# A two-layer product behind a retention block: two levels of Strassen for the first product of four chunks

## The chip, the cores and the metric

One NeuronCore of one Trainium2 chip runs one program. The metric is the time of that program on the device in microseconds. The engines are TensorE (PE, with its weight loads listed apart as PEld), VectorE (DVE), ScalarE (ACT), GpSimd (POOL) and the DMA queues, which SyncE (SP) issues.

## What is computed

All tensors are fp32; the weights arrive as 64-bit floats and are converted on the chip.

```python
q, k, v: (4, 8, 768, 64)          # batch, heads, time, head dim
w_in: (512, 2048)   w_out: (2048, 512)

for t in range(S):                # retention, one decay gamma[h] per head
    state = gamma * state + outer(k[:, :, t], v[:, :, t])
    y[:, :, t] = scale * q[:, :, t] @ state
x = y.transpose(0, 2, 1, 3).reshape(3072, 512)
h = x @ w_in                      # first product
g = maximum(0.01 * h, h)          # leaky relu
return g @ w_out                  # second product
```

## The kernel before

**Chunks and units.** Time is cut into NC = 6 chunks of C = 128 steps. A chunk has 4 batches, thus 512 tokens, which the products take as two halves of N = 256 columns. The 2048 hidden features are cut into NU = 4 units of 512. `hidden(c, u, ...)` (L615) makes unit u of the first product for chunk c, and `output(c, o, parts, ...)` (L650) adds the second product of one or two units into the chunk's output tile `o`.

**One level of Strassen.** Each product is a 2 by 2 block product in the form with seven products, M1 to M7, and three differences of either side. `seven` (L561) issues the matmuls: each of the seven has four of 128x128 weights by 256 columns, so a call has 28 for one unit and 56 for a pair. The sums go to four PSUM banks A to D, each a tile of its own (tag "ff", four buffers): M1 and M2 share A, M6 and M7 share B, M5 and M3 share C, M4 has D. After each of the seven, `takes` evacuates or adds: a ScalarE copy for M1 and M5, VectorE adds (`plus`, L526) for the others, a ScalarE leaky relu for each quarter of `g`. `differences` (L544) makes the three differences of `x` or `g` on VectorE. Weight sums (`add_sums`, L532) are made once on VectorE and stay in SBUF.

**Attention.** `reads`, `last_values`, `state`, `first_values` and `score` put 64-column and 128-column matmuls of the retention block into a pair of banks (`two_banks`, L158, tag "att", two buffers). `visit_with_scores` (L380) does two batches of a chunk in one go, with the scores of the two batches that come next.

**Order.** The schedule is written by hand: each engine executes its instructions in the order in which the code issues them. Chunks 0 and 1 go unit by unit while the weights still arrive and are converted (`round_piece`, L480). Chunks 2 to 5 then run `hidden`, `hidden`, `output` of the pair, twice a chunk, with the attention of the next chunk between. SP issues every load and store in program order, so a DMA that waits holds back those behind it.

Of the kernel before, what the change touches and what calls it, by code (L numbers as in the profile page):

```python
# [21 lines left out]

@with_exitstack
def kernel(
# [14 lines left out]

# [12 lines left out]
        tc.tile_pool(name="psum", bufs=2, space=bass.MemoryType.PSUM))  # L75

# [6 lines left out]

# [5 lines left out]
    def unit_tile(k, name):  # L91
        if k in LATE:
            return work.tile([128, 7, 2, 256], FP32, tag=f"late{k}", name=name)
        return const.tile([128, 7, 2, 256], FP32, name=name)
# [21 lines left out]

# [50 lines left out]

# [15 lines left out]
    def new_am(c, b):  # L187

        i = turn[0]
        turn[0] = (i + 1) % (3 if (c, b) >= (2, 2) else 2)  # L190
        if i < 2:
            return work.tile([128, 2, HP // 2, 3, C // 2], FP32, tag=f"am{i}", name=f"am_{c}_{b}")
        place = new_t(1, f"am_{c}_{b}").rearrange("p i k n -> p (i k n)")[:, 0 : 2 * NS]
        return place.rearrange("p (j m n t) -> p j m n t", j=2, n=3, t=C // 2)

    def new_t(c, name):
        return work.tile([128, 3, 2, N], FP32, tag=f"t{int(c == 1)}", name=name)
# [13 lines left out]


    pairs = [(j, m, i, 2 * m + i) for m in range(HP // 2) for j in range(2) for i in range(2)]

    def reads(c, b):
        x = heads[c, b][0]
        ps = sums_at[c, b] = two_banks(f"yp_{c}_{b}")
        for j, m, i, a in pairs:
            mm = nc.tensor.matmul(ps[ts(i, 64), j, m, :], lhsT=st[b][ts(j, 64), a, :],  # L219
                                  rhs=x[ts(j, 64), 0, a, :], start=(m == 0), stop=False,  # L220
                                  skip_group_check=True)


        reads_done[c, b] = nc.gpsimd.memset(between, 0.0).ins
        tc.add_manual_dep(reads_done[c, b], mm.ins.name, IN_ORDER, reason="rows of the array")
# [48 lines left out]
    def first_state(b, ps):  # L274


        y = heads[0, b][1]
        sp = ps[:, b // 2].rearrange("p a t -> p (a t)")[:, ds(b % 2 * HP * D, HP * D)]
        for a in range(HP):
            sums_of(sp.rearrange("p (a d) -> p a d", d=D), y, a, start=(b % 2 == 0 and a == 0))  # L280
# [35 lines left out]
    def ahead(c, b):  # L316


        if c >= NC:
            return  # L320
        if b < 2:
            x = work.tile([128, 2, HP, C], FP32, tag="qk", bufs=AHEAD, name=f"qk_{c}_{b}")
        else:
            if b == 2:
                room[c] = new_o(0).rearrange("p i k n -> p (i k n)")
            x = room[c][:, ds((b - 2) * 2 * HP * C, 2 * HP * C)]
            x = x.rearrange("p (s a t) -> p s a t", s=2, a=HP)
        heads[c, b] = [x, None]
        load_qk(c, b)
# [8 lines left out]
    def score_apart(c, b):  # L338

        banks = [psum.tile([128, HP * C], FP32, tag="ff", bufs=4, name=f"ap{j}_{c}_{b}")[:, 0:NS]  # L340
                 for j in range(2)]
        scores[c, b] = [ps.rearrange("p (m n t) -> p m n t", n=3, t=C // 2) for ps in banks]
        scores_to(heads[c, b][0], scores[c, b])
# [14 lines left out]
    def states_apart(c, b):  # L358

        ps = psum.tile([128, 2, HP, D], FP32, tag="ff", bufs=4, name=f"sp_{c}_{b}")  # L360
        for i in range(2):
            y = heads.pop((c, b + i))[1]
            for a in range(HP):
                sums_of(ps[:, i], y, a, start=(i == 0 and a == 0))
        return ps

    def visit(c, b):

        for f in (reads, last_values, state, first_values):
            for i in range(2):  # L370
                f(c, b + i)
        for i in range(2):
            tokens_taken(c, b + i, xs[c][0])
        for i in range(2):
            state_taken(c, b + i, for_state(sums_at[c, b + i]))
        for i in range(2):
            if c + 1 < NC:
                ahead(c + 1, b + i)

    def visit_with_scores(c, b, following, complete=False):  # L380

        x = xs[c][0]
        early, late = ((following[0], following[1] + i) for i in range(2))
        score_apart(*early)
        for i in range(2):
            reads(c, b + i)
        masked_apart(*early, 0)
        masked_apart(*early, 1)  # L390
        score_apart(*late)
        for f in (first_values, last_values):
            for i in range(2):
                f(c, b + i)
        masked_apart(*late, 0)
        for i in range(2):
            tokens_taken(c, b + i, x)
        sp = states_apart(c, b)
        if complete:
            if xs[c][1] is None:  # L400
                xs[c][1] = new_t(c, f"t_{c}")
            t = xs[c][1]
            for k in range(2):
                minus(t[:, 0, k], x[:, 1, k], x[:, 0, k])
                minus(t[:, 1, k], x[:, 3, k], t[:, 0, k])
        masked_apart(*late, 1)
        if complete:
            minus(t[:, 2], x[:, 2], t[:, 1])
        for i in range(2):
            state_added(c, b + i, sp[:, i])  # L410
        if complete:
            last_difference(x)
        for i in range(2):
            state_decayed(c, b + i)
        for i in range(2):
            ahead(c + 1, b + i)
        for at in (early, late):
            load_kv(*at)
        for at in (early, late):
            decay_v(*at)  # L420

# [67 lines left out]

# [3 lines left out]

# [7 lines left out]


# [50 lines left out]

# [5 lines left out]
    def seven(tiles, name, takes, takes_piece=None, order=ORDER):  # L561

        banks = {}
        which = [("M1", "A", 0, 0), ("M6", "B", 5, 5), ("M5", "C", 4, 4), ("M4", "D", 3, 6),
                 ("M2", "A", 2, 2), ("M7", "B", 1, 1), ("M3", "C", 6, 3)]
        for m, bank, sa, sb in (which[i] for i in order):
            first = bank not in banks  # L570
            split = takes_piece is not None and bank == "C"
            if first and split:
                two = [two_banks(f"{bank}{i}_{name}")[:, 0].rearrange("p a t -> p (a t)")
                       for i in range(2)]
                two.append(psum.tile([128, 2 * N], FP32, tag="ff", bufs=4, name=f"{bank}_{name}"))
                banks[bank] = [ps[:, 0 : z - a] for ps, (_, a, z) in zip(two, PIECES)]
            elif first:
                banks[bank] = psum.tile([128, 2, N], FP32, tag="ff", bufs=4, name=f"{bank}_{name}")
# [19 lines left out]
    def direct(c, u, x, g, th):  # L598


        banks = [psum.tile([128, 2, N], FP32, tag="ff", bufs=4, name=f"d{r}_{c}_{th}")
# [48 lines left out]
    def output(c, o, parts, first, final):  # L650
# [48 lines left out]
        def takes_piece(ps, i, a, z):  # L699
# [4 lines left out]
                     takes_piece if final and c == NC - 1 else None)  # L704

# [4 lines left out]
    def new_x(c):  # L710
        x = tile_x(c)
        return [x, new_t(c, f"t_{c}") if c < 3 else None]
# [76 lines left out]


# [3 lines left out]


    idle = psum.tile([128, 2, N], FP32, tag="ff", bufs=4, name="idle")
# [7 lines left out]

    tables = psum.tile([128, 2, N], FP32, tag="ff", bufs=4, name="tables")
    spread = psum.tile([128, 2, N], FP32, tag="ff", bufs=4, name="spread")
# [71 lines left out]


# [38 lines left out]


    for u in range(NU):
        for c in range(2) if u > 0 else ():
            if c == 0:
                parts = []
            parts.append(new_g(c, u))
            run(hidden(c, u, *xs[c], *parts[c][1:]), rounds(1, 3))
        for c in range(2):
# [5 lines left out]
            if u == NU - 1 and NC > 2:  # L934
                if c == 0:
                    xs[2] = new_x(2)
                if c == 0:
                    at = {0: [scored(2, 0), scored(2, 1)], 3: [lambda: visit(2, 0)]}
                else:
                    at = {1: [lambda: ahead(2, 2), lambda: ahead(2, 3)],  # L940
                          2: [lambda: load_kv(2, 2), lambda: load_kv(2, 3)],
                          4: [scored(2, 2), scored(2, 3)]}
            run(output(c, os[c], [parts[c]], u == 0, u == NU - 1), at)

    if NC > 2:
        visit_with_scores(2, 2, (3, 0), complete=True)
    for c in range(2, NC):
        os[c] = new_o(c)
        for p in range(NU // 2):
            pair = []  # L950
            for u in (2 * p, 2 * p + 1):
                pair.append(new_g(c, u))
                run(hidden(c, u, *xs[c], *pair[-1][1:]), {})
            last = p == NU // 2 - 1
            at = {}
            if c + 2 == NC and last:
                at = {3: [lambda: visit(c + 1, 2)], 5: [differ(c + 1)]}
            run(output(c, os[c], pair, p == 0, last), at)

            if c + 1 < NC and p == 0:  # L960
                xs[c + 1] = new_x(c + 1)
                visit_with_scores(c + 1, 0, (c + 1, 2))
            elif c + 2 < NC and last:
                visit_with_scores(c + 1, 2, (c + 2, 0), complete=True)
# [3 lines left out]

# [5 lines left out]

def _decay(H, D):

# [13 lines left out]

# [33 lines left out]

# [30 lines left out]
```

## Time and profile before

| what | value |
|---|---|
| median of 3 runs | 657.06 us (657.01 to 657.62) |
| profiled execution, its span | 655.4 us |
| instructions of PE / DVE / ACT / POOL | 4937 / 590 / 323 / 45 |
| busy time of DVE, ACT, POOL | 361.5, 176.1, 22.7 us |
| one add of 128x512 on DVE | 0.68 to 0.69 us |
| one copy of 128x512 from PSUM on ACT | 0.58 to 0.59 us |
| HBM read, written | 41.97 MB, 6.29 MB |

The span runs from the first to the last instruction of the profiled execution. An fp32 matmul stands in the trace as two records, each with a weight load of its own. A record lasts longer than its distance to the next one (379 ns beside 216 ns for 256 columns), since they are pipelined; the distance is what a matmul costs. "Idle before" is what an engine waited, with the engine that ended the wait.

### The profile page before, as it was taken

To read this page: it belongs to the slowest core of one execution; us is meant where nothing else is said; L and a number is where in the kernel's file an instruction comes from. 1 tells how busy PE (TensorE), PEld (TensorE's weight loads), DVE (VectorE), ACT (ScalarE), POOL (GpSimd) and SP (SyncE) were. 2 spreads that over 40 slices of the span, in tenths; PEclk is the share of its full clock that TensorE was granted. 3 is DMA by queue.
4 is the path that set the end of the run, shared out by engine and by line. 5 is a ranking of instruction groups with operands and counts; after the bars stand their busy time and mean duration, and the time that the engine had idled before them with its cause. 6 is when DMAs were issued, how large, how long until landed. Compare 5 with 4: busy or idle time off the path is not lost.

```text
span 655.4 us, 11361 instructions
## 1 busy us (share of the span) xinstructions
PE 650.6 (99%) x4937; PEld 568.2 (87%) x4937; DVE 361.5 (55%) x590; ACT 176.1 (27%) x323; POOL 22.7 (3%) x45
## 2 busy tenths in 40 slices
PE   8999999999999999999999999999999999999998
PEld 5888888888888888888888889888888888888887
DVE  5789969889887664243436414527423344431342
ACT  5855464264261003102102211300220210221210
POOL 1000000000000020000001001001000100000000
DMA  9921312323322650030022003005001001000001
GB/s 337 406 98 37 125 64 97 97 66 111 115 78 82 243 179 0 1 129 2 1 103 91 1 1 130 1 17 179 0 1 61 5 1 49 17 0 1 1 0 65
DMA packets 15906, 49.00 MB, mean 75 GB/s; under 512 B 1768, under 2 KB 2152, under 8 KB 15856
## 3 DMA queue, kind: packets, MB, share of 16 engines
q1 hardware_dynamic: 15696, 47.72, 20.7%
q8 instruction: 39, 0.64, 0.4%
q10 hardware_dynamic: 160, 0.55, 0.2%
q14 instruction: 11, 0.09, 0.0%
HBM read 41.97 MB, written 6.29 MB: 74 GB/s over the span
## 4 chain that ended last, share of the span: by engine, by line
PE 98%; DMA 1%; DVE 0%; ACT 0%; SPq 0%; issue 0%
PE B_o L585 13%; PE A_o L585 13%; PE C_o L585 13%; PE A_h L585 12%; PE B_h L585 12%; PE C_h L585 12%; PE D_o L585 6%; PE D_h L585 6%; PE ap L182 2%; PE d L607 2%; PE yp L255 2%; PE yp L219 1%; DMA raw<-in_weights_dram 1%; PE yp L244 1%; PE sp L270 1%; PE yp L270 0%
## 5 line engine op out<-in xcount | busy, mean ns | idle before, releaser
L585 PE MATMUL A_h<-x,w 128*128 128x256 f32 x368 | 87.7, 381 | 0.0
L585 PEld LDWEIGHTS A_h<-x,w 128*128 128x128 f32 x368 | 69.3, 190 | 9.6
L585 PE MATMUL A_o<-g,w 128*128 128x256 f32 x288 | 68.1, 379 | 0.0
L527 DVE TENSOR_TENSOR m<-m,B_h 128x512 f32<-128x512 f32 x23 | 15.8, 686 | 93.3 <-PE B_h L585 93.3
L585 PEld LDWEIGHTS A_o<-g,w 128*128 128x128 f32 x288 | 54.6, 190 | 7.5
L620 ACT ACTIVATE g<-g 128x512 f32<-128x512 f32 x69 | 42.0, 630 | 66.3 <-DVE g L527 66.3
L625 ACT COPY m<-A_h 128x512 f32<-128x512 f32 x23 | 13.5, 585 | 169.3 <-PE A_h L585 149.0
L527 DVE TENSOR_TENSOR m<-m,B_o 128x512 f32<-128x512 f32 x16 | 11.0, 685 | 64.4 <-PE B_o L585 64.4
L585 PE MATMUL B_h<-t,w 128*128 128x256 f32 x184 | 43.7, 380 | 0.0
L585 PE MATMUL C_h<-x,w 128*128 128x256 f32 x184 | 43.5, 379 | 0.0
L585 PE MATMUL C_h<-t,w 128*128 128x256 f32 x184 | 43.5, 379 | 0.0
L585 PE MATMUL D_h<-t,w 128*128 128x256 f32 x184 | 43.5, 379 | 0.0
L585 PE MATMUL B_h<-x,w 128*128 128x256 f32 x184 | 43.5, 379 | 0.0
L585 PEld LDWEIGHTS B_h<-t,w 128*128 128x128 f32 x184 | 34.7, 190 | 5.2 <-DVE t L530 0.6
L585 PEld LDWEIGHTS C_h<-x,w 128*128 128x128 f32 x184 | 35.0, 190 | 4.8
L585 PEld LDWEIGHTS D_h<-t,w 128*128 128x128 f32 x184 | 35.0, 190 | 4.8
L585 PEld LDWEIGHTS C_h<-t,w 128*128 128x128 f32 x184 | 35.0, 190 | 4.8
L585 PEld LDWEIGHTS B_h<-x,w 128*128 128x128 f32 x184 | 35.0, 190 | 4.8
L585 PE MATMUL C_o<-gd,w 128*128 128x256 f32 (+1 forms) x148 | 34.2, 373 | 0.0
L585 PE MATMUL C_o<-g,w 128*128 128x256 f32 (+1 forms) x148 | 34.2, 373 | 0.0
L530 DVE TENSOR_TENSOR gd<-g,gd 128x512 f32<-128x512 f32 x48 | 33.2, 692 | 1.7
L585 PE MATMUL B_o<-gd,w 128*128 128x256 f32 x144 | 34.1, 380 | 0.0
(131 smaller groups left out, 984.6 us busy)
## 6 DMA issues: line engine op xcount, KB each, us to landing
raw<-in_weights_dram SPq DMA_DIRECT2D x31, 512.0 KB, 3.9
kv<-in_kv_dram SPq DMA_DIRECT2D x17, 512.0 KB, 5.0
out_dram<-o SPq DMA_DIRECT2D x23, 256.0 KB, 2.1
qk<-in_qk_dram SPq DMA_DIRECT2D x10, 512.0 KB, 4.6
o<-in_qk_dram SPq DMA_DIRECT2D x8, 512.0 KB, 4.9
in<-in_qk_dram SPq DMA_DIRECT2D x5, 512.0 KB, 8.4
in<-in_kv_dram SPq DMA_DIRECT2D x3, 512.0 KB, 7.9
kv<-in_kv_dram SPq DMA_DIRECT2D x4, 256.0 KB, 7.4
```

Of the source, the lines that this page charges most:

```text
L182: nc.tensor.matmul(to, lhsT=x[ts(j, 64), 1, a, ts(late, 64)], rhs=x[ts(j, 64), 0, a, late * 64 :])
L219: mm = nc.tensor.matmul(ps[ts(i, 64), j, m, :], lhsT=st[b][ts(j, 64), a, :], rhs=x[ts(j, 64), 0, a, :], start=(m == 0), stop=False, skip_g ...
L244: mm = nc.tensor.matmul(ps[ts(i, 64), j, m, 0:64], lhsT=y[ts(s, 64), 1, 2 * a + j, :], rhs=am[ts(s, 64), j, m, 0], start=False, stop=True, ...
L255: nc.tensor.matmul(ps[ts(i, 64), j, m, 64:], lhsT=y[:, 1, 2 * a + j, :], rhs=am[:, j, m, 1 + (i ^ j)], start=(c == 0 and m == 0), stop=Tru ...
L270: nc.tensor.matmul(sp[ts(j, 64), a, :], lhsT=y[:, 0, 2 * a + j, :], rhs=y[:, 1, 2 * a + j, :], start=start, stop=True, skip_group_check=True)
L527: nc.vector.tensor_tensor(out=out, in0=a, in1=b, op=ALU.add)
L530: nc.vector.tensor_tensor(out=out, in0=a, in1=b, op=ALU.subtract)
L585: nc.tensor.matmul(to, lhsT=block(w, sa)[:, k, ts(i, 128)], rhs=rhs[:, k, a:z], start=(first and (i == 0 or split) and n == 0 and k == 0), ...
L607: nc.tensor.matmul(banks[r][:, i, :], lhsT=block(2 * u, r + 2 * kh)[:, k, ts(i, 128)], rhs=x[:, 2 * kh + th, k, :], start=(step == 0 and i ...
L620: nc.scalar.activation(g[:, i], g[:, i], AF.Prelu, alpha=0.01)
L625: nc.scalar.copy(out=got["m1"], in_=ps)
```

## The change

The first product of chunks 2 to 5 goes from one to two levels of Strassen. `hidden` is used there no more; `inner` and `outer` take its place, in two groups: group 0 makes four of the seven outer products, group 1 the other three. In `inner` each outer product is again seven products, each one matmul of 128x128 weights by 128 columns, so a group has 28 or 21 matmuls. All of it goes to one PSUM tile, `whole`, of four banks: the bank is the quarter of the inner result, the place in the bank is the outer product. A ScalarE copy puts M1 from bank 0 into bank 3, onto which later matmuls accumulate; three VectorE adds per group finish the inner sums in PSUM. `outer` does what `takes` did.

The second weight sums are made on GpSimd from the first while chunks 0 and 1 run (`sums_of_unit`), stored to DRAM (`keep_unit`), and loaded for each chunk and unit again (`load_unit`, 14 KB and 10.5 KB a partition, in two transfers each, into `wa` and `wb`). `output` is called unit by unit and takes its four banks from two tiles of two banks each (`att_banks`). The attention uses `joint_visit`, with its scores in `whole`. The main loop handles unit n of the second product while unit n+1 of the first is made.

```diff
-    def seven(tiles, name, takes, takes_piece=None, order=ORDER):
+    def att_banks(name):
+        ab, cd = (two_banks(f"{n}_{name}").rearrange("p j a t -> p j (a t)") for n in ("ab", "cd"))
+        return [ps.rearrange("p (i n) -> p i n", i=2)
+                for ps in (ab[:, 0], ab[:, 1], cd[:, 0], cd[:, 1])]
+    def seven(tiles, name, takes, takes_piece=None, order=ORDER, room=None):
...
+            elif first and room is not None:
+                banks[bank] = at[bank]
             elif first:
-                banks[bank] = psum.tile([128, 2, N], FP32, tag="ff", bufs=4, name=f"{bank}_{name}")
+                banks[bank] = ffs.tile([128, 2, N], FP32, tag="ff", bufs=4, name=f"{bank}_{name}")
...
+    def joint_visit(c, b, following):
+        for f in (reads, last_values, state, first_values):
             for i in range(2):
                 f(c, b + i)
+        ahead_of = [(following[0], following[1] + i) for i in range(2)] if following else []
+        for i, at in enumerate(ahead_of):
+            score_apart(*at, banks=[whole[:, q] for q in (2 * i, 2 * i + 1)])
         for i in range(2):
+            tokens_taken(c, b + i, xs[c][0])
+        for at in ahead_of:
+            for j in range(2):
+                masked_apart(*at, j)
         for i in range(2):
+            state_taken(c, b + i, for_state(sums_at[c, b + i]))
+            heads.pop((c, b + i))
...
+    def sums_of_unit(u):
...
+        for to, p, q, op in ((s1, a21, a22, ALU.add), (s2, s1, a11, ALU.subtract),
+                             (s4, a12, s2, ALU.subtract), (s3, a11, a21, ALU.subtract)):
+            nc.gpsimd.tensor_tensor(out=to, in0=p, in1=q, op=op)
...
+    def keep_unit(u):
+        for j, part in enumerate(to_keep.pop(u)):
+            nc.sync.dma_start(out=kept[u][:, j], in_=part)
...
+    whole = ctx.enter_context(
+        tc.tile_pool(name="whole", bufs=1, space=bass.MemoryType.PSUM)).tile(
+            [128, 4, 4 * C], FP32, name="whole")
+    regions = whole.rearrange("p q (i n) -> p q i n", i=4)
...
+    INNER = {"M1": (0, 0), "M2": (1, 1), "M4": (2, 4), "M5": (3, 2), "M6": (4, 3), "M3": (5, 5),
+             "M7": (6, 6)}
+    BANK = {"M1": 0, "M2": 0, "M5": 1, "M3": 1, "M4": 2, "M6": 3, "M7": 3}
+    N2 = (NC - 2) * NU
...
+    def load_unit(n, group):
...
+        if group == 0:
+            nc.sync.dma_start(out=wa[:, :, 0:1], in_=kept[u][:, :, 0:1])
+            nc.sync.dma_start(out=wa[:, :, 1:4], in_=kept[u][:, :, 3:6])
+        else:
+            nc.sync.dma_start(out=wb[:, :, 0:2], in_=kept[u][:, :, 1:3])
+            nc.sync.dma_start(out=wb[:, :, 2:3], in_=kept[u][:, :, 6:7])
...
+    def sums_of_x(c, group):
...
+            minus(made[:, 0], b12, b11)
+            minus(made[:, 1], b22, made[:, 0])
+            minus(made[:, 2], b21, made[:, 1])
+            minus(b12, b22, b12)
+    ORDERS = (("M1", "M5", "M6", "M4", "M2", "M7", "M3"), ("M1", "M5", "M4", "M6", "M2", "M3", "M7"))
+    def inner(n, group):
+        c, u = at_of(n)
+        w, count = ((wa, 4), (wb, 3))[group]
+        moving = operands(c, group)
+        def of(q):
+            return regions[:, q, 0:count]
+        t2, t3, t5 = e2[:, 0:count], e3[:, 0:count], e5[:, 0:count]
+        for m in ORDERS[group]:
+            j, s = INNER[m]
+            q = BANK[m]
+            for i, (block, sums) in enumerate(moving):
...
+                nc.tensor.matmul(regions[:, q, i], lhsT=w[:, j, i], rhs=rhs,
+                                 start=(i == 0 and m in ("M1", "M5", "M4")), stop=True,
+                                 skip_group_check=True)
+            if m == "M1":
+                nc.scalar.copy(out=of(3), in_=of(0))
+            elif m == "M5":
+                nc.scalar.copy(out=t5, in_=of(1))
+            elif m == "M6":
+                nc.scalar.copy(out=t2, in_=of(3))
+            elif m == "M7":
+                nc.scalar.copy(out=t3, in_=of(3))
+        load_unit(n + 1, group)
+        plus(of(3), of(3), t5)
+        plus(of(2), of(2), t3)
+        plus(of(1), of(1), t2)
+    def outer(n, group):
+        if group == 0:
+            nc.scalar.copy(out=m1, in_=regions[:, :, 0])
+            plus(u2, m1, regions[:, :, 3])
+            nc.scalar.copy(out=m5, in_=regions[:, :, 2])
+            nc.scalar.copy(out=m4, in_=regions[:, :, 1])
+            plus(u5, u2, m5)
+            return
+        gs[n] = new_g(*at_of(n))
+        g = gs[n][1]
...
+        plus(to(0), m1, regions[:, :, 1])
+        leaky(0)
+        plus(u2, u2, regions[:, :, 0])
+        plus(to(1), u5, regions[:, :, 2])
+        leaky(1)
+        plus(to(3), u2, m5)
+        leaky(3)
+        plus(to(2), u2, m4)
+        leaky(2)
...
+    for group in range(2):
+        load_unit(0, group)
+    x, t = xs[2]
+    differences(x, t)
+    sums_of_x(2, 0)
+    sums_of_x(2, 1)
+    for b in range(2):
+        ahead(3, b)
+        load_kv(3, b)
+        decay_v(3, b)
...
+    last = output(1, os[1], [parts[1]], False, True, room=att_banks)
+    products(last, 3)
+    for i in range(2):
+        score_apart(3, i, banks=[whole[:, q] for q in (2 * i, 2 * i + 1)])
+        for j in range(2):
+            masked_apart(3, i, j)
+    for b in range(2):
+        ahead(3, 2 + b)
+    fill()
+    inner(0, 0)
+    outer(0, 0)
+    products(last, 2)
+    inner(0, 1)
+    outer(0, 1)
+    products(last, 2)
+    for n in range(N2):
...
+        if more:
+            differences(*gs[n][1:])
+        if u == NU - 1 and more:
+            sums_of_x(c + 1, 1)
+        if more:
+            inner(n + 1, 0)
+            outer(n + 1, 0)
+        if c + 1 < NC and u < 2:
...
+                joint_visit(c + 1, 0, (c + 1, 2))
...
+        steps = output(c, os[c], [gs.pop(n)], u == 0, u == NU - 1,
+                       room=att_banks if more else whole_banks, order=ORDER if more else FIRST)
+        products(steps, 4)
+        if c + 1 < NC and u < 2:
+            fill()
...
+        if more:
+            inner(n + 1, 1)
+            outer(n + 1, 1)
+        if n + 2 == N2:
+            differences(*gs[n + 1][1:])
+        products(steps, 3)
```

`products(steps, n)` issues the next n of the seven products of `output`; `fill` is one bf16 matmul of 512 columns into bank 3 of `whole`.

## The prediction

> **What bounds the kernel now.** I read the busy shares first, then stretches without attention, then the pace of matmuls by shape.
>
> ```profile
> PE 650.6 (99%) x4937; PEld 568.2 (87%) x4937; DVE 361.5 (55%) x590; ACT 176.1 (27%) x323; POOL 22.7 (3%) x45
> ```
>
> TensorE is busy for 99% of the span, and the chain that ended last is 98% PE. In a stretch of chunk 2 without attention (view of stretches; columns: PE, PEld, DVE, ACT, POOL):
>
> ```profile
> 291.00:338.00 47.00, 47.00 (x219) 41.37 (x219) 18.97 (x31) 7.77 (x13) 2.08 (x2) 1.00 0.09 32
> ```
>
> PE has no gap, DVE works 40% and ACT 17% of it. So only TensorE's time counts, and a wait put before a matmul is paid in full unless other matmuls stand ahead of it in PE's order. The pace (timeline of PE, first 256 columns, then 128):
>
> ```profile
> 337.22 1.03 PE L585 MATMUL C_o<-g,w 128*128 128x256 f32 x4
> 338.08 1.03 PE L585 MATMUL C_o<-g,last_s 128*128 128x256 f32 x4
> ```
>
> ```profile
> 650.66 0.61 PE L585 MATMUL C_o<-g,w 128*128 128x128 f32 x4
> 651.10 0.61 PE L585 MATMUL C_o<-g,last_s 128*128 128x128 f32 x4
> 651.55 0.61 PE L585 MATMUL C_o<-g,w 128*128 128x128 f32 x4
> 652.00 0.61 PE L585 MATMUL C_o<-g,last_s 128*128 128x128 f32 x4
> ```
>
> Four records of 256 columns start 0.86 us apart, thus 216 ns each; four of 128 columns 0.446 us apart, thus 111.5 ns, each with its own 128x128 weight load. Halving the columns halves the price: weight loads do not bound the new shape. An fp32 matmul is two records: 0.432 and 0.223 us.
>
> **What the change removes on PE.** Per chunk and unit the first product goes from 28 matmuls of 256 columns (12.10 us) to 28 + 21 of 128 (6.24 + 4.69 = 10.93 us): 1.17 us less, 16 times, **-18.7 us**. The second product keeps its 28 matmuls a unit, and the attention its number. Seven `fill` matmuls come in, 0.25 us each with weight load: **+1.8 us**.
>
> **What it adds: turns.** In the order of the changed program with the wait that each instruction carries, the matmuls of `inner` do not only wait for what they need. `whole` is one tile, and after each ScalarE access to it the next matmul into it waits, whichever bank it writes. In group 0, M5 waits for the copy after M1, M6 for the copy after M5, M4 for that after M6, M3 for that after M7: four turns PE to ACT to PE with nothing ahead of them. Group 1 has three (M5, M4, M2). In `output` the banks A, B are one tile and C, D another: M6 waits for the copy after M1, M4 for the add after M5, M7 for the add after M2. Before, each bank was a tile of its own, and the copies lay beside the next product.
>
> One turn, from rows:
>
> ```profile
> L625 ACT COPY m<-A_h 128x512 f32<-128x512 f32 x23 | 13.5, 585 | 169.3 <-PE A_h L585 149.0
> L527 DVE TENSOR_TENSOR m<-m,B_h 128x512 f32<-128x512 f32 x23 | 15.8, 686 | 93.3 <-PE B_h L585 93.3
> L620 ACT ACTIVATE g<-g 128x512 f32<-128x512 f32 x69 | 42.0, 630 | 66.3 <-DVE g L527 66.3
> ```
>
> A record outlasts its pace by 0.16 us (275 - 111.5, or 379 - 216 ns); ACT or DVE starts 0.04 us after its end; the matmul starts 0.055 us after the release (as `d` at L607 after the DVE row on w), and the weight load, no longer hidden, shows as 0.104 us (that first record is 320 ns from the next, not 216). So a turn costs its operation plus 0.36 us. The copy of 512: 0.585 + 0.36 = 0.945 us. Of 384, on the line between 12 columns (0.168 us) and 512: 0.48 + 0.36 = 0.84. An add on DVE: 1.05. No row shows ACT or DVE writing PSUM: a copy there costs between the 0.168 us of the 12-column copy and the 0.63 of the leaky relu, an add between the 0.553 us of the 384-column mask and the 0.95 of the 768-column one. I take the same-sized rows.
>
> **One step of the loop without attention** (n = 2, 3, 6, 7 and on). Two waits are longer than a turn, since they stand behind a queue.
>
> - `inner` group 0: 4 x 0.945 = 3.8 us.
> - `output` M6 waits for the copy of M1, which is fourth in ACT's order. From the end T of group 0: 0.2, three adds in PSUM (2.07), copy m1 (0.62), add u2 (0.72), copies m5 and m4 (1.2), the copy itself (0.58), release 0.16: T + 5.56. M1 alone covers 1.73: 3.8 us.
> - M4 behind DVE's add: 1.05 us.
> - `inner` group 1: 3 x 0.84 = 2.5 us.
> - M7 waits for DVE's add of M2. From the end of group 1: 0.2, ACT's copy 0.48, three adds of 384 (1.66), five of `outer` (3.45), the add (0.69), release 0.16: 6.67 us. M2 alone covers 1.73: 4.9 us.
>
> Together 16.1 us of idle PE beside 23.0 us of work: a step of 39.1 us. Fifteen steps: 241.5 us. In the four first steps of a chunk M2 goes through ACT behind a leaky relu: +0.5 each. In the six steps with attention the scores wait for `outer`'s copy m4 (about 1.2 us), M1 of `output` for masks and states (3.0), while M6 falls to 0.95: 1.5 us more than without, each. **Stalls of the loop: +252 us.**
>
> **The change-over** (end of chunk 1). Weights of unit 0 are issued behind the last store of output(0, 3). By DMA rows (27 ns for 512 B, 48 for 1 KB, 16 engines) they take 9.5 us, and the qk and kv of chunk 3 stand behind them on SP: the second score can start about 20 us after the visit, of which M3, M1, M6 and M5 cover 8. With its mask 14 us of idle. Then the turns and waits of the first `inner` pair (3.8 + 1.5 + 2.5), M6's 0.95, and a slow clock of some 2 us: **+25 us**, between 12 (qk lands early) and 35. **The end**: the last M7 of step 14 stands behind four differences (+3), and the last `output` has four turns in `whole` (+4): **+7 us**.
>
> **Hidden.** Weight loads in the loop: 3.2 MB a step, 9.5 us by the packet rows (24 at the 131 GB/s of a raw load, 512 KB in 3.9 us), issued some 29 us ahead of their use. DVE has 17.5 us of adds a step of 39: late only where named. GpSimd's sixteen sums of 896 columns (1.9 us each from the 1.09 us of 512) and the stores fall into chunks 0 and 1, where DVE is busy 43.7 of 50 us; an add beside a GpSimd operation took 684 ns, beside none 686. I cost them at nothing; if raw loads are held behind the stores, up to 10.
>
> **The clock.** The trace shows what an idle PE does to it:
>
> ```profile
> 1.05 4.45 PE L800 MATMUL idle<-t 128*128 128x512 bf16 x10 [1.05 <-DVE t L764]
> 12.26 0.39 PE L800 MATMUL idle<-t 128*128 128x512 bf16 x1
> ```
>
> The first ten are 427 ns apart, twice the later pace of such columns (256 fp32 columns in two passes: 216), for at least 4.4 us: one re-warming costs 2.2 us. The trace has no gap of 3 to 5 us in mid-run; the longest near it, 0.4 us before `d`, left the clock high. Two gaps of each step (3.8 and 4.9 us) may trigger it: 0 to 30 x 2.2 = 66 us. The seven turns near 0.9 us resemble the 0.4 us gap; so I take few events, one of the longer gaps in three: **+12 us**.
>
> The Trainium skill ("TensorE: Matmul & The Clock Gate", Part 1) says that a free-running window of 3.4 us without work sets the clock to half until a busy one has passed. By that a 4.9 us gap holds such a window in 4 of 10 cases and a 3.8 us gap in 1 of 10; at an estimated 1.7 us each the sum would get 13 us instead of 12. The same skill ("PSUM — Partial Sum Buffer", PSUM bank collisions) asks engines to be kept apart bank by bank only; by that rule most turns are needless and the sum would be near that of the first rival. The waits are in the program, though, and the hardware obeys them.
>
> **Sum.** 655.4 - 18.7 + 1.8 + 252 + 25 + 7 + 12 = 934.5 us of span; the median stands 1.7 above the span: **936 us**.
>
> **Rivals.**
> 1. *PE works on during the turns* (not slower). If matmuls queued ahead made each turn cost nothing, the 18.7 us would count: 655.4 - 18.7 + 1.8 + 12 (change-over) + 1.7 = 652 us, faster by 0.7%. The point of decision: all losses together 16.9 us (18.7 - 1.8), about 1.1 us a step, against 16 here. For it: DVE and ACT would have room. Against: PE's order is fixed, and the waiting matmul is the next one each time. 5%.
> 2. *The clock falls for long*: both long gaps re-warm every time and the dense turns delay it: 936 + 54 = 990 us, up to 1040 with 5 us of slow products after each. For it: the first rows above. Against: no such gap in the trace. 22%.
> 3. *PE stays at half clock throughout the loop*, since it works 59% of it: 15 x 23 us more, near 1280. 5%.
> 4. *Shorter turns*: PSUM writes cost little and the change-over's loads come early: 8 x 16 x 0.1 for the operations and 13 for the change-over, near 905 us. 18%.
>
> **How the numbers follow.** My forecast has 50%, from 915 to 960. The range of eight in ten takes in the fourth rival and the first part of the second: 890 to 1000 us. Below 0.2%, what a measurement of this kernel can tell from none, I call it the same: faster 4%, same 1%, slower 95%.
>
> **What will show it.** Right: PE busy near 64% of the span; PE waits on ACT `whole` about 0.9 us long, some 110 times; on DVE `o` for M7 near 5 us, 15 times; PE records of 128 columns 111.5 ns apart between turns; a step of 39 us. Wrong: 128-column records 223 ns apart (clock); PE waiting for DMA of `wa` or `wb` in the loop (loads); M5 starting right behind M1 (rival 1).

## The result and the profile after

The changed kernel takes 1008.54 us (median, 1004.06 to 1015.23) against 657.20 us before (657.01 to 657.62): a ratio of 1.535, 95% interval 1.529 to 1.541. The forecast was 936 us, its range 890 to 1000. The direction and the cause were foreseen, the size was not: the profiled execution took 1004.06 us (span 1002.3), 68 us more than the sum.

First the busy shares and the granted clock from the page of the changed kernel:

```profile
PE 751.3 (75%) x5576; PEld 629.6 (63%) x5576; DVE 532.1 (53%) x832; ACT 254.8 (25%) x475; POOL 60.0 (6%) x61
PEclk9999999999587888989999988989899989989989
```

PE falls from 99% to 75%. The granted clock was 1.00 in every stretch of the kernel before; here its line has dips all along the loop. The view of stretches, in two parts of the loop without attention (two steps, then four; PE, PEld, DVE, ACT, POOL, granted clock, DMA share, GB/s):

```profile
585.83:671.39 85.56, 59.02 (x310) 49.18 (x309) 38.76 (x64) 17.68 (x32) 0.00 (x0) 0.90 0.25 79
764.79:935.58 170.79, 117.28 (x618) 97.87 (x617) 69.76 (x113) 37.01 (x67) 0.00 (x0) 0.90 0.26 82
```

A step takes 42.7 us, not 39.1, at a mean clock of 0.90. DVE is at 41 to 45% and ACT at 21 to 22% of it: neither is short of time. What PE waits for in the loop (view of waits, PE, from 300 to 960 us: total, times, longest):

```profile
PE ab_o L518 <- DVE o L455: 43.6, 10, 4.4
PE ab_o L518 <- ACT m L594: 36.4, 15, 3.6
PE ab_o L518 <- ACT o L616: 19.6, 4, 4.9
PE whole L983 <- ACT temps L989: 19.2, 28, 1.0
PE whole L983 <- ACT temps L991: 18.1, 29, 0.7
PE whole L983 <- ACT whole L987: 17.7, 28, 0.7
...
PE whole L983 <- ACT wb L993: 10.1, 15, 0.7
PE cd_o L518 <- DVE m L455: 8.6, 11, 0.8
```

These are the turns of the prediction, with its releasers: M7 behind the add or copy of M2 (14 times), M6 behind the copy of M1 (15), `inner` behind ScalarE's copies (100 times; the tile `wb` of L993 is one that a copy writes). No row waits for a transfer into `wa` or `wb`. What the prediction did not have shows in the timeline of PE in one of these steps:

```profile
775.14 1.89 PE L518 MATMUL ab_o<-g,w 128*128 128x256 f32 x8
780.62 3.47 PE L518 MATMUL ab_o<-gd,w 128*128 128x256 f32 x8 [3.59 <-ACT m L594]
783.93 1.89 PE L518 MATMUL cd_o<-gd,w 128*128 128x256 f32 x8
786.60 1.99 PE L518 MATMUL cd_o<-gd,w 128*128 128x256 f32 x8 [0.78 <-DVE m L455]
...
795.71 1.89 PE L518 MATMUL ab_o<-g,w 128*128 128x256 f32 x8
801.96 3.78 PE L518 MATMUL ab_o<-g,w 128*128 128x256 f32 x8 [4.36 <-DVE o L455]
805.54 2.88 PE L518 MATMUL cd_o<-g,w 128*128 128x256 f32 x8
```

The same eight records take 1.89 us, or 3.47 and 3.78 us right behind a gap of 3.59 or 4.36 us; behind the gap of 0.78 us they take 1.99. The trace's record of the clock has 32 stretches at half, 179.8 us in all: one of 27.31 us at the change-over, then 3.41, 6.83 or 10.24 us each, and one that the program's end cuts off. In them records of 256 columns stand 427 ns apart, not 216, and those of 128 columns 213 ns, not 112. Beside the same records at full clock (my estimate, from their distances) that costs about 67 us, some 7 of them at the change-over. The sum had 14.

The second loss lies before the loop. DVE at 46 us, and GpSimd beside it:

```profile
44.76 1.27 DVE L458 TENSOR_TENSOR t<-x 128x512 f32<-128x512 f32 x1
46.06 4.93 DVE L458 TENSOR_TENSOR t<-x,t 128x512 f32<-128x512 f32 x2
50.92 0.68 DVE L458 TENSOR_TENSOR x<-x 128x512 f32<-128x512 f32 x1
```

```profile
43.06 2.42 POOL L857 TENSOR_TENSOR sum<-sum,w 128x896 f32<-128x896 f32 x1
45.55 2.41 POOL L857 TENSOR_TENSOR sum<-w,sum 128x896 f32<-128x896 f32 x1
47.92 2.52 POOL L857 TENSOR_TENSOR sum<-w 128x896 f32<-128x896 f32 x1
```

Two differences of 0.69 us each take 4.93 us together; the third, once GpSimd's sums have ended, takes 0.68. PE's M6 waits 1.65 us there. Operations that read PSUM beside a sum keep their length (`x<-yp,dec`: 674 and 678 ns, 686 without a sum). Gaps of this kind add up to some 13 us before the loop.

### The profile page after: what moved, and what is told of

Read it like the earlier page. It is cut to its first block, busy times and chain, and to the rows that moved or that the text cites. A ratio compares the mean times of both kernels' runs of the same rounds, so it can differ in the third digit from the quotient of the medians.

```text
span 1002.3 us, 13268 instructions
## 1 busy us (share of the span) xinstructions
PE 751.3 (75%) x5576; PEld 629.6 (63%) x5576; DVE 532.1 (53%) x832; ACT 254.8 (25%) x475; POOL 60.0 (6%) x61
## 4 chain that ended last, share of the span: by engine, by line
PE 58%; DVE 23%; ACT 13%; issue 4%; DMA 2%; ACTq 0%; DVEq 0%
PE whole L983 22%; PE ab_o L518 12%; PE cd_o L518 9%; DVE whole L455 6%; DVE g L455 3%; PE C_o L518 2%; DVE temps L455 2%; DVE o L455 2%; PE B_o L518 2%; ACT temps L989 2%; ACT wb L993 2%; ACT temps L991 2%; PE A_o L518 2%; ACT whole L987 2%; DVE m L455 1%
## 5 line engine op out<-in xcount | busy, mean ns | idle before, releaser
L455 DVE TENSOR_TENSOR whole<-whole,temps 128x512 f32<-128x512 f32 (+1 forms) x64 | 40.5, 633 | 227.5 <-ACT wb L993 114.3
L518 PE MATMUL ab_o<-g,w 128*128 128x256 f32 x288 | 96.7, 495 | 70.4 <-DVE o L455 37.7
L518 PEld LDWEIGHTS ab_o<-g,w 128*128 128x128 f32 x288 | 69.1, 252 | 87.8 <-DVE o L455 40.9
L983 PE MATMUL whole<-x,wa 128*128 128x128 f32 x512 | 87.1, 308 | 45.6 <-ACT temps L989 12.0
L983 PE MATMUL whole<-x,wb 128*128 128x128 f32 x672 | 90.4, 282 | 30.1 <-ACT temps L989 10.0
L983 PEld LDWEIGHTS whole<-x,wa 128*128 128x128 f32 x512 | 72.5, 208 | 60.7 <-ACT temps L989 15.3
L983 PEld LDWEIGHTS whole<-x,wb 128*128 128x128 f32 x672 | 81.0, 191 | 41.0 <-ACT temps L989 13.0
L983 PE MATMUL whole<-t,wa 128*128 128x128 f32 x384 | 57.0, 288 | 0.0
L518 PE MATMUL cd_o<-gd,w 128*128 128x256 f32 x192 | 48.8, 399 | 8.9 <-DVE m L455 6.2
L983 PEld LDWEIGHTS whole<-t,wa 128*128 128x128 f32 x384 | 51.9, 205 | 0.0
L993 ACT COPY wb<-whole 128x512 f32<-128x512 f32 (+1 forms) x32 | 17.0, 533 | 92.7 <-PE whole L983 92.7
```

The source lines that it names most:

```text
L455: nc.vector.tensor_tensor(out=out, in0=a, in1=b, op=ALU.add)
L518: nc.tensor.matmul(to, lhsT=block(w, sa)[:, k, ts(i, 128)], rhs=rhs[:, k, a:z], start=(first and (i == 0 or split) and n == 0 and k == 0), ...
L983: nc.tensor.matmul(regions[:, q, i], lhsT=w[:, j, i], rhs=rhs, start=(i == 0 and m in ("M1", "M5", "M4")), stop=True, skip_group_check=True)
L993: nc.scalar.copy(out=t3, in_=of(3))
```

## The experiments

Theory T: the time is PE's work, plus turns because several banks are one tile, plus a half clock after each long gap, plus DVE held by GpSimd, plus a change-over that waits for loads in queue order.

### 1. Fillers in the two long gaps (T against "the clock has another cause")

```diff
+            for _ in range((warm or {}).get(m, 0)):
+                nc.tensor.matmul(at["D"].rearrange("p i (h n) -> p (i h) n", h=2), lhsT=filled,
+                                 rhs=filled.unsqueeze(1).to_broadcast([128, 4, C]), start=True,
+                                 stop=True, skip_group_check=True)
             ps = banks[bank]
...
+                       warm={"M6": 16, "M7": 21} if more else None)
```

> Edit: in the loop, 16 throwaway bf16 matmuls of 512 columns (0.216 us each, 3.5 us) ahead of output's M6 and 21 (4.5 us) ahead of its M7, into bank D of cd, which nothing waits for then; they run inside the two long gaps (3.8 and 4.9 us) that the trace of the changed kernel shows, so no wait is taken away. Theory T (a step is 23.0 us of matmuls plus 16.1 us of turns, and 3.5 us more because the clock halves after each long gap): half-clock time in the loop all but goes, a step falls from 42.7 to 39.2 us, the total to 950 us (943 to 962). Rival R1 (the step is set by weight loads, DVE or ACT, and the clock falls where PE waits anyway): step and total stay, 1000 to 1012. Rival R2 (the clock halves of itself under this pattern of short fp32 matmuls, gaps or not): half-clock time stays near 150 us and the total rises, 1004 to 1030.

Measured 961.92 us (961.57 to 964.54), ratio 1.464 (1.462 to 1.466): 46.6 us less than the changed kernel, with no wait removed. Two steps of it without attention in the view of stretches, and the two places in the timeline:

```profile
570.63:648.53 77.90, 66.99 (x384) 50.96 (x383) 38.65 (x65) 17.68 (x32) 0.00 (x0) 1.00 0.28 87
```

```profile
582.71 3.62 PE L513 MATMUL cd_o<-mask 128*128 128x512 bf16 x16
586.46 1.99 PE L522 MATMUL ab_o<-gd,w 128*128 128x256 f32 x8
...
601.80 4.70 PE L513 MATMUL cd_o<-mask 128*128 128x512 bf16 x21
606.34 1.99 PE L522 MATMUL ab_o<-g,w 128*128 128x256 f32 x8
```

The clock is 1.00, M6 and M7 start where they started before, and the eight records behind them take 1.99 us. A step is 38.95 us: the forecast's 39.1. R1 and R2 fall.

In the six steps with attention, though, the gap that the fillers ahead of M6 were meant for is not there. M6 of such a step in the changed kernel, and with the same fillers in the trace of experiment 12:

```profile
510.48 1.99 PE L518 MATMUL ab_o<-gd,w 128*128 128x256 f32 x8 [0.68 <-ACT m L594]
```

```profile
473.53 3.62 PE L513 MATMUL cd_o<-mask 128*128 128x512 bf16 x16
476.99 1.89 PE L522 MATMUL ab_o<-gd,w 128*128 128x256 f32 x8
```

There M6 starts 3.29 us behind M1 instead of 0.68: the fillers cost 2.6 us a step at full clock, 15.7 us in all. So the half clock cost more than the 46.6 us, and the total lies at the upper end of T's range.

### 2 and 3. Where the clock falls: gaps of 1.6 and of 2.5 us

The same edit with fewer fillers, `{"M6": 9, "M7": 14}` and `{"M6": 5, "M7": 9}`.

> Edit: as the kernel with fillers, but only 9 ahead of M6 and 14 ahead of M7, so that about 1.6 us (M6) and 1.3 to 1.9 us (M7) of each gap stay idle. In the traces so far every PE gap of 3.59 us or more (24 of 24) was followed by half clock, of those between 2.0 and 3.0 us about half, of those up to 1.7 us none that had not another cause. Theory W (the clock halves when a window of some 1.7 us that runs on its own is wholly idle: 2.5/1.7 - 1 is about the half seen): no half clock after these gaps, steps of 39.0 us, total 962 (955 to 968), as with all gaps filled. Rival V (the mean load over a few us counts, and a gap of 1.6 in 3.6 us already lowers it): half clock returns after some of them, total 970 to 1000.

> Edit: as the kernel with fillers, but 5 ahead of M6 and 9 ahead of M7: about 2.5 us (M6) and 2.4 to 3.0 us (M7) of each gap stay idle. Theory W: a gap of 2.5 us holds a wholly idle window of 1.7 us in (2.5 - 1.7)/1.7, about 0.5 of the cases: 10 to 17 of the 29 gaps lead to half clock, of 3.4 us or 6.8 us each, and the total stands between 962 and 1008, at 980 (972 to 992). Rival V (no sharp window, load counts): either nearly none or nearly all of these gaps lead to half clock, 962 to 968 or 1000 to 1010.

Measured 961.05 us (954.23 to 962.89), ratio 1.459 (1.454 to 1.465), and 978.24 us (975.30 to 985.50), ratio 1.490 (1.483 to 1.497). M6 in the timeline of the one and of the other:

```profile
579.38 2.00 PE L522 MATMUL ab_o<-gd,w 128*128 128x256 f32 x8 [1.65 <-ACT m L598]
```

```profile
587.97 3.63 PE L522 MATMUL ab_o<-gd,w 128*128 128x256 f32 x8 [2.51 <-ACT m L598]
```

Counted over the traces, PE's long gaps in the loop, nine ahead of M6 (steps without attention) and fourteen ahead of M7, from the end of a record to the next start, and how many were followed by half clock:

| kernel | length of the gaps, us | number | half clock follows |
|---|---|---|---|
| changed | 3.59 to 4.90 | 23 | 23 |
| sums left out (below) | 3.59 to 4.90 | 23 | 23 |
| fillers 5 and 9 | 2.41 to 2.95 | 23 | 15 |
| fillers 9 and 14 | 1.33 to 1.88 | 23 | 0 |

In these profiled executions a gap of up to 1.9 us cost no clock, one of 2.4 to 3.0 us did in two cases of three, one of 3.6 us always. V, in the form that a gap of 1.6 us already lowers the clock, falls. Theory W foretold the times (0 below 1.7, about half, all above 3.4), but the record of the clock shows another rule than its idle window of 1.7 us. In each trace the half-clock stretches start whole multiples of 3.413 us apart, so the clock goes by fixed slots of this length. Of the 23 gaps with 5 and 9 fillers the 15 that were followed by half clock began 0.2 to 1.3 us after the start of a slot, the other eight 1.6 to 2.2 us after it, so that the next slot got part of their idle time. All slots of the thirteen traces that have such stretches (from 20 us on, idle from the end of a record to the next start):

| clock in the slot | idle PE in it, us | slots | half clock in the next slot |
|---|---|---|---|
| full | under 1.68 | 2650 | 0 |
| full | 1.68 to 2.0 | 43 | 18 |
| full | over 2.0 | 132 | 132 |
| half | under 0.56 | 134 | 0 |
| half | 0.56 to 0.8 | 37 | 31 |
| half | over 0.8 | 65 | 65 |

It is the idle time of a slot in all that counts: ten slots of 1.68 to 1.92 us idle lost the clock with no gap above 1.2 us in them. And a clock that is at half mostly stays there for another slot over an idle time as short as one turn.

### 4 and 5. Banks apart: first the output's, then `whole` too

```diff
     def two_banks(name):
+        if second:
+            return [second[0].tile([128, HP, C], FP32, tag="att", bufs=4, name=f"{name}_{j}")
+                    for j in range(2)]
```

```diff
-            [128, 4, 4 * C], FP32, name="whole")
+    whole = [pool.tile([128, 4 * C], FP32, name=f"whole{q}") for q in range(4)]
...
+    def copied(to, i):
+        for q in range(4):
+            nc.scalar.copy(out=to[:, q], in_=regions[q][:, i])
```

> Edit: from the change-over on, the pairs of banks ab, cd and those of the visits become tiles of one bank each (four buffers); tokens_taken reads two tiles in two instructions. Nothing else changes. Theory T (a matmul waits for the last reader of its tile, whichever bank it read, and a long gap costs clock): the waits of M6 (3.8), M4 (1.05) and M7 (4.9) go, and with them the half clock; a step is 42.7 - 9.8 - 3.5 = 29.4 us, the total 1004 - 15 x 13.3 = 805 us (790 to 830). Rival R1 (weight loads, DVE or ACT set the step and the waits are only where it shows): the gaps come back elsewhere, total above 900. Rival R3 (the turns go but DVE's queue, filled for a step of 39 us, is late next): 830 to 900, with gaps at inner's first matmuls.

> Edit: as the kernel with banks apart, and `whole` is four tiles of one bank too; the outer level's seven operations over the four banks become four of 128 columns each (12 more on ACT and 12 more on DVE per step... outer has three copies on ACT and four additions on DVE). Theory T: the turns of 0.84 to 0.95 us inside the inner products go as well; a step is its matmuls and what little is left, 23.5 to 25 us; total 1004 - 15 x 18.5 = 727 us (705 to 750). Rival R3 (DVE and ACT, with the added instructions, are late next): a step of 27 to 31 us, total 770 to 840. Rival R1 (loads of weights bound the step): no better than the kernel with the output banks apart.

Measured 812.93 us (810.65 to 822.77), ratio 1.239 (1.232 to 1.247), and 698.63 us (697.38 to 702.86), ratio 1.065 (1.061 to 1.069). Two steps of each in the view of stretches:

```profile
638.37:697.22 58.85, 49.77 (x310) 44.21 (x309) 38.13 (x65) 17.69 (x33) 0.00 (x0) 1.00 0.37 110
```

```profile
554.95:601.22 46.27, 46.27 (x310) 43.31 (x309) 38.52 (x89) 18.46 (x51) 0.00 (x0) 1.00 0.45 140
```

Steps of 29.43 and 23.14 us, where T had 29.4 and 23.5 to 25. With eight banks apart PE has no gap in the step, though DVE is at 83% of it and works through twelve more instructions. The timeline of PE in that kernel, group 0 and the first products of `output`:

```profile
578.61 0.83 PE L995 MATMUL whole<-t,wa 128*128 128x128 f32 x6
579.28 3.17 PE L995 MATMUL whole<-x,wa 128*128 128x128 f32 x26
...
584.75 1.89 PE L529 MATMUL ab_o<-g,last 128*128 128x256 f32 x8
586.47 1.89 PE L529 MATMUL ab_o<-gd,last 128*128 128x256 f32 x8
```

M5, M6 and M4 run through where three turns stood. The rivals R1 and R3 fall; the total came out 6 us below my lower end, since I had left up to 2 us of waits in a step.

### 6 and 7. GpSimd's sums: left out, and in pieces

The first, on the changed kernel, stores plain quarters in place of the sums; the second, on the kernel with eight banks apart, computes the same sums in 128-column pieces.

```diff
-            nc.gpsimd.tensor_tensor(out=to, in0=p, in1=q, op=op)
+            for i in range(7):
+                nc.gpsimd.tensor_tensor(out=to[:, i], in0=p[:, i], in1=q[:, i], op=op)
```

> Edit: GpSimd's sums of weight quarters (16 additions of 896 columns) are left out and plain quarters are stored in their place, so chunks 2 to 5 are computed from wrong weights; the stores, the loads and all that follows are the same. Theory T (while these additions run, DVE's operations between two SBUF operands take up to 2.5 us instead of 0.7, and the first part waits for them, 13 us in all): the last output of the first part starts 11 to 15 us earlier, the total is 991 (986 to 995). Rival R4 (the stores to DRAM, or the split of the load work, cost these 13 us): the first part stays within 3 us and the total within 4 us.

> Edit: as the kernel with all eight banks apart (698.6 us), and each of GpSimd's 16 additions of 896 columns is issued as 7 of 128 columns; the results are the same. Theory H (a DVE operation between SBUF operands waits until the GpSimd instruction under way has ended, up to 2.5 us): DVE is held for one short piece at most, and 8 to 12 of the 13 us lost in the first part come back; total 689 (684 to 693). Rival S (the two engines share the port by turns, so what counts is GpSimd's total work, which this raises): nothing comes back or more is lost, total 698 to 708.

Sums left out: 996.52 us (990.96 to 999.74), ratio 1.515 (1.509 to 1.521), 12.0 us less than the changed kernel, and the first `inner` starts 12.85 us earlier (248.25, not 261.10 us). Median 1.5 us above T's upper end; R4 falls. In pieces: 687.39 us (686.86 to 689.01), ratio 1.046 (1.044 to 1.047), 11.2 us less than without. The two differences of above, left out and in pieces, and GpSimd in pieces:

```profile
45.34 1.42 DVE L458 TENSOR_TENSOR t<-x,t 128x512 f32<-128x512 f32 x2
```

```profile
45.58 1.69 DVE L470 TENSOR_TENSOR t<-x,t 128x512 f32<-128x512 f32 x2
```

```profile
44.55 4.92 POOL L869 TENSOR_TENSOR sum<-sum,w 128x128 f32<-128x128 f32 x7
49.43 4.65 POOL L869 TENSOR_TENSOR sum<-w,sum 128x128 f32<-128x128 f32 x7
```

4.93 us becomes 1.69. GpSimd needs up to twice as long (4.92 for what took 2.42 us), and nothing waits for GpSimd. So it is the length of the single instruction that DVE pays for (H), not the total (S).

The Trainium skill ("SBUF — State Buffer", "SBUF: two separate sides") says it so: a GpSimd operation and a DVE operation with two SBUF inputs share a pair of ports, whichever starts first holds it for its whole instruction, and the other waits. This trace agrees: 2.45 us instead of 0.69 beside sums of 2.1 to 2.5 us.

### 8. The change-over: q and k ahead of the weight sums

On the kernel with eight banks apart.

```diff
+    for b in range(2):
+        ahead(3, b)
     for group in range(2):
         load_unit(0, group)
+    for b in range(2):
+        load_kv(3, b)
...
     for b in range(2):
-        ahead(3, b)
-        load_kv(3, b)
         decay_v(3, b)
```

> Edit: as the kernel with all eight banks apart, and at the change-over the loads of chunk 3's q and k for two scores (1 MB) are issued ahead of the first unit's 3.1 MB of weight sums, v after them. Theory T (PE's wait of 9.7 us there is the wait for a transfer that stands behind the weights in the queue): the scores start 6 us earlier, the first inner product then waits some 2 to 4 us for its weights; total -4 us (-2 to -7), 694. Rival (the transfers start late because their buffers come free late, order apart): within 1.5 us of 698.6.

Measured 690.40 us (689.89 to 693.77), ratio 1.051 (1.048 to 1.053): 8.2 us less, 1.2 more than I had allowed. Waits of PE from 225 to 270 us, without and with the edit:

```profile
PE whole L160 <- DMA qk<-in_qk_dram: 10.6, 2, 9.7
PE whole L1068 <- DVE am L324: 1.1, 1, 1.1
```

```profile
PE whole L1070 <- DVE am L324: 5.2, 1, 5.2
...
PE whole L160 <- DMA qk<-in_qk_dram: 0.3, 1, 0.3
```

The wait for the transfer was its place in the queue; next late are the masks, behind DVE's sums of x.

### 9 to 11. All three together, loads left out, and an attempt at the rest

> Edit: eight banks apart, GpSimd's additions in pieces of 128 columns and chunk 3's q and k ahead of the weight sums, all three together. If the losses are separate, they add up: 698.6 - 11.2 - 8.2 = 679 us (676 to 682). Rival (the two share a cause, for instance the clock at the change-over): 682 to 687.

> Edit: as the kernel with all three, and the weight sums are loaded for the first unit only (15 of 16 loads of 3.1 MB left out, 48 MB), so all later units compute with the first unit's weights. Theory T (the loads land beside PE's work and cost nothing, as the prediction had it): within 2 us of the kernel with the loads. Rival R1 (they contend for SBUF or delay q, k and v): 4 to 15 us faster.

```diff
     def load_unit(n, group):
-        if n >= N2:
+        if n >= 1:
             return
```

> Edit: as the kernel with all three, and (a) chunk 3's first two scores are taken after the first part's last output, in its banks, not ahead of the first inner product; (b) five, not three, of the last but one output's products are held back to cover the chain of DVE and ACT ahead of the last output. Theory T: the gap of 4.7 us before the last output and its half clock go for the most part (-4 to -7), the 5.2 us that the first inner product waits for the masks go, partly replaced by 2 us at the scores (-2 to -6): 669 (664 to 674), and so still 1 to 2 per cent slower than the kernel before (657). Rival (DVE's queue in these places is full and the waits only move): 675 to 680.

```diff
-        products(steps, 4)
+        products(steps, 2 if n + 2 == N2 else 4)
...
-    products(last, 3)
-    for i in range(2):
-        score_apart(3, i, banks=[whole[q] for q in (2 * i, 2 * i + 1)])
+    products(last, 4)
+    fill()
+    inner(0, 0)
...
+    for i in range(2):
+        pair = two_banks(f"ap_3_{i}")
```

All three: 681.01 us (679.33 to 682.67), ratio 1.036 (1.034 to 1.038); the sum of the parts was 679.2, so the losses are separate.

Loads for the first unit only: 674.66 us (672.48 to 676.72), ratio 1.026 (1.024 to 1.028), 6.3 us faster: T missed. Waits of PE in the loop, with the loads and without:

```profile
PE whole L160 <- issue: 3.8, 3, 2.4
PE ab_o L529 <- issue: 2.9, 1, 2.9
PE ab_o L529 <- DVE x L272: 1.3, 1, 1.3
```

```profile
PE whole L160 <- issue: 1.9, 1, 1.9
PE ab_o L529 <- DVE x L272: 1.3, 1, 1.3
```

The plain step is 23.14 us in both. What goes are waits at the scores and at the M1 behind a visit (4.8 us). The half-clock stretch of 3.41 us behind the longest goes too, but another comes elsewhere; both traces have 18 us of half clock in all. The rows name `issue`, not a transfer of q or k, and the longest falls inside M1, behind its first record. In ten of the traces PE has 18 such waits above 1 us behind 230 us. At each of them a packet of a DMA queue for instructions (q8, some 44 packets in a whole trace) starts between 1.4 us before the wait and 0.6 us after its start, while the 16 DMA engines are full. So PE may wait there for its own instructions behind the weights; no run tried it by itself.

The last attempt: 683.94 us (683.04 to 686.85), ratio 1.041 (1.039 to 1.043), no better. PE at the change-over (view of waits, 225 to 285 us):

```profile
PE whole L996 <- DMA wa<-kept: 4.6, 2, 3.3
PE whole L160 <- issue: 3.0, 1, 3.0
PE ap L160 <- DVE m L467: 2.0, 1, 2.0
PE ap L160 <- DVE o L467: 1.5, 1, 1.5
```

The first product now comes before its weights have landed, and the scores wait for DVE: the waits only moved. The gap ahead of the last output fell from 4.75 to 2.15 and 0.68 us, and what that saved went there. So the best version stands at 681 us, 3.6% above the kernel before.

### 12. All turns kept, three losses taken out

The changed kernel, all turns kept, with the fillers of 1, the pieces of 7 and the order of 8.

> Edit: the changed kernel with its tiles and turns as they are, plus the fillers ahead of M6 and M7, GpSimd's additions in pieces of 128 columns, and chunk 3's q and k ahead of the weight sums. It takes out what the forecast of 936 us left out or sized too small and keeps every turn. If the three losses are separate: 961.9 - 11.2 - 8.2 = 942.5 us (937 to 948), close to the forecast's own sum. Rival (the losses overlap, so the forecast's turns are too small as well): 950 to 962.

Measured 948.72 us (938.56 to 957.45), ratio 1.439 (1.434 to 1.445): on the edge between the two. The executions differ with the clock that they were granted: 938.56 us at 0.987, 949.99 at 0.972, and the profiled one 940.91 at 0.985 with 30.4 us of half clock. On that line a clock of 1.00 would give some 929 us (my estimate).

This kernel is not quite the one that the forecast added up. Its fillers cost 15.7 us in the steps with attention (experiment 1), and the forecast had counted the wait for q and k, which the order of 8 shortens by 8.2 us. Without the fillers' share it would take 929 - 15.7 = 913 us; the forecast without its half clock and without the 8.2 us is 936 - 14 - 8.2 = 914 us. So the rest of the sum, its turns, long waits, steps with attention and change-over taken together, was right to within a few us, or errors in it cancel.

## Why the prediction failed

**The step that failed** is "so I take few events, one of the longer gaps in three: +12 us". Every gap of 3.59 to 4.90 us ahead of M6 and M7 in the loop (23 of 23) halved the clock, for 3.41 or 6.83 us each. With 2 us in the change-over the sum had 14 us of half clock; the records show about 67. Filling the gaps takes 46.6 us back, net of what the fillers cost. The mechanism was named and its frequency was mis-sized; the second rival (both gaps every time, 990 us) was the nearest case, and my range stopped 8.5 us short of the result since I gave that rival only its first part. Its other half, that the dense turns delay the warming, came true in part: turns alone did not lower a full clock as long as a slot held under 1.68 us of them, but they kept a halved one down. In the changed kernel 21 of 52 slots at half clock were followed by another, and the stretch at the change-over lasted 27.31 us, with all banks apart 13.65.

The skill misled me here by my choice of passage. "TensorE: Matmul & The Clock Gate", Part 1, gives the idle window as 3.4 us, and I worked out hits in 1 of 10 and 4 of 10 cases; measured are 23 of 23, and 15 of 23 at 2.4 to 3.0 us. The same part ("HAM oscillation — how this bites in real kernels") tells of waits of some 3 to 5 us, each of which starts the next burst cold, every time. That is what this trace shows, and the quanta of 3.41 us agree with the page. A window wholly without work was not needed here: over 2.0 us idle in a slot of 3.41 us were enough (132 of 132).

**The second failed step** is GpSimd at nothing: "an add beside a GpSimd operation took 684 ns, beside none 686", with "up to 10" if raw loads are held. The cost was 12 to 13 us, and the cause another. With both steps put right the sum comes out: 934.5 + 53 (half clock, 67 - 14) + 12.85 = 1000 us beside the span of 1002.3. My row was an addition that reads PSUM (`u<-m,B_h`). The trace of before had one that spoke against it (all `states` products by form: shortest, median, longest):

```profile
L313 DVE TENSOR_TENSOR states<-states,dec x16: 418/420/1266, 35.1 to 455.5; 128x256 f32<-128x256 f32 x16
```

Two SBUF operands, 420 ns as a rule, 1266 ns once, beside GpSimd products of 1.18 and 1.11 us. I read a mean over the wrong kind of operand.

**What held.**
- *Turns and step.* 39.1 us forecast, 38.95 with the clock kept (experiment 1). Taking the waits at M6, M4 and M7 away brought 29.43 us, taking those in `inner` away 23.14, beside the 23.0 of work. The tile, not the bank, was what made matmuls wait.
- *Pace.* 216 and 112 ns at full clock.
- *The change-over.* PE waited 11.0 us there for q and k and twice 1.2 us for the masks, 13.4 us beside the 14 of the forecast. That q and k wait behind the weights is shown by experiment 8 (8.2 us).
- *Loads.* Hidden in a step; up to 6 us at visits, seen in a faster kernel only. The fourth rival's terms (936 - 12.8 - 13) give 910 us, not 905; nothing rests on it.
- *Rival 1* (652 us). Even with every bank apart and two more repairs the time is 681 us: the turns hid a change-over, visits and an end that the 18.7 us saved do not pay for.

**The signs to look for.** Waits on ACT in `whole` came 100 times in the loop, near the 110 foretold; as idle time they show 0.57 to 0.73 us, since the record outlasts its pace by 0.16 and the bare weight load stands in the record. M7's waits came 14 times, 4.4 or 4.9 us. PE busy is 75%, not 64%: records that outlast their pace count as busy before each turn, and half clock makes them longer. That sign was badly chosen; the length of a step and the pace of the records were the good ones.

The end (+7) was not measured by itself; of its parts, the last M7 of the loop waited 7.16 us, where the forecast had 4.9 + 3.

## What to carry to other kernels

Ask of each gap that a change puts into TensorE's stream not only how long it is but whether it costs clock behind it: fill it, or break it, before counting on full pace, and put no filler where the gap is not there. Give every PSUM bank its own tile where matmuls of one bank should run beside reads of another; here that alone was worth 310 us of 350. When judging whether an engine can work "beside" another, compare operations of the same operand kind, and look at the longest of a group, not at its mean.

## What the runs showed of the hardware that I had not expected

- Half clock comes in slots of 3.41 us, 2 to 5 us after the gap begins: in the loop behind none of 23 gaps of 1.33 to 1.88 us and behind all 46 of 3.59 to 4.90 us. Between them the gap's place on the slots decides: over 2.0 us idle in one slot lost the clock (132 of 132).
- PE 85% busy, with gaps of about 0.7 us every 2 us in `inner`, keeps the full clock (first kernel of experiments 4 and 5, 1.00 over two steps); at half clock 0.6 to 0.8 us idle in a slot mostly kept it there (29 of 34).
- GpSimd's additions of 896 columns hold DVE's SBUF operations for up to 2.5 us; seven pieces of 128 columns hold them by 0.14 to 0.26 us each, and GpSimd itself slows from 2.4 to 4.9 us.
- A throwaway matmul makes a kernel faster: 37 per step, 8 us of PE time that for the most part was idle, took 46.6 us off.
